# Second batch transposed in 64-column tiles without reordering copies, padding written behind the bias table, fewer 256-column units

## The chip, the cores and the metric

The kernel runs on one core of one Trainium2 chip. The metric is the device time of one execution in microseconds (us). The clock that TensorE was granted differs from one execution to the next, and this moves the time by up to about 1%. Small differences are therefore read from several rounds on one chip, never from one pair of runs. The record counts ratios within 2% as the same; smaller differences are read here from the 95% intervals.

The engines are called by their short names: PE is TensorE, PEld its weight loads, DVE is VectorE, ACT is ScalarE, POOL is GpSimd, SP is SyncE.

## The reference

Eight batches and eight heads of attention over 576 tokens, with 64 dimensions per head and a bias that depends only on the distance of query and key, are followed by a gated feed-forward layer over all 4608 tokens.

```python
scores = scale * q @ k.T                         # 8 x 8 x 576 x 576
scores = scores + bias_table[bucket(|i - j|)]    # 32 buckets, one column per head
attn   = softmax(scores)
x      = (attn @ v).transpose(...).reshape(4608, 512)
out    = ((x @ w_a) * (x @ w_b)) @ w_out         # d_ff = 1536
```

The kernel works on "pairs": pair p holds two heads of one batch, so pairs 0 to 3 are the first batch, pairs 4 to 7 the second. The 576 tokens are split in 512 and a "tail" of 64.

## The kernel before

`vt` holds the tail's values, one tile for even batches and one for odd. Head 0 of a pair lies in partitions 0 to 63, head 1 in partitions 64 to 127, each beside zeros, and each has a column of ones that gives the sum for the softmax:

```python
vt = [wpool.tile([128, H // 2, 2, Dh + 1], BF16, name=f"vt{i}") for i in range(2)]

def load_vt(b):
    for hh in range(2):
        nc.gpsimd.dma_start(
            out=vt[b % 2][64 * hh:64 * hh + 64, :, hh, 0:Dh],
            in_=v[b, hh:H:2, SM:S, :].transpose([1, 0, 2]))

def padding():
    for i in range(2):                                            # tails of q and k
        nc.vector.memset(tl[i][0:64, :, :, Dh:], 0.0)
        nc.vector.memset(tl[i][64:128, :, :, 0:Dh], 0.0)
    for i in range(2):                                            # tails of v
        nc.vector.memset(vt[i][0:64, :, 1, :], 0.0)
        nc.vector.memset(vt[i][64:128, :, 0, :], 0.0)
        nc.vector.memset(vt[i][0:64, :, 0, Dh:Dh + 1], 1.0)
        nc.vector.memset(vt[i][64:128, :, 1, Dh:Dh + 1], 1.0)
```

The order of the start, with the rest cut:

```python
nc.vector.memset(zero_sb[:, :], 0.0)
nc.vector.memset(tab_sb[0:H, :], 1.0)
nc.vector.tensor_tensor(out=bt_sb..., op=subtract)
padding()                                      # 12 memsets on DVE, ahead of all loads of q, k and v
for h in range(0, H, 2):
    load_q(0, h, h + 2)
    load_k(0, h, h + 2)
load_tails(0)
load_v(0, 0, 4)
load_vt(0)
...                                            # weights and the second batch, issued by POOL
load_vt(1)
...
warm_up(5)                                     # matmuls on zeros
nc.scalar.activation(out=eb_sb..., in_=bt_sb..., func=ACTF.Exp)
nc.tensor.matmul(out=tps..., lhsT=eb_sb..., rhs=oh_sb...)          # the bias table
warm_up(2)
nc.vector.tensor_copy(out=tab_sb[0:H, c0:c0 + NR], in_=tps[0:H, 0:NR])
nc.sync.dma_start(out=tab.ap(), in_=tab_sb[0:H, :])
for hp in range(H // 2):
    nc.sync.dma_start(out=W_sb[hp]..., in_=<a sliding view of tab>)
    if hp == 0:
        ...                                    # two loads of Wt_sb
...
t_qk(0)                                        # transposes of q and k, copies to QT and KT
t_qk(1)
scores0(0, 0)                                  # first score matmuls and exponentials
warm_up(2)
t_qk(2)
...
```

The first batch is transposed in eight 64-column matmuls per pair for each of q and k. The second batch is first brought into another order by DVE copies and is then transposed in four full ones:

```python
def transposes(ps, src, p, tag):
    b, hp = divmod(p, 4)
    for t in range(NM):
        if b == 0:
            for hh in range(2):
                o = 256 * (2 * hp + hh) + 64 * t
                nc.tensor.transpose(ps[64 * hh:64 * hh + 64, 128 * t:128 * t + 128],
                                    src[0][:, o:o + 64], ident[:, :])
        else:
            nc.tensor.transpose(ps[:, 128 * t:128 * t + 128], st[p][tag][:, t, :, :], ident[:, :])
```

The softmax here doesn't subtract the row's maximum and nothing guards it: scores larger than these inputs give would overflow.

## Time and profile before

| | before |
|---|---|
| median of 3 runs | 436.58 us (436.36 to 438.47) |
| span of the profiled run | 434.6 us, granted clock 0.998 |
| PE busy | 414.3 us, 95% |
| DVE busy, ACT busy | 242.3 us, 248.4 us |
| first score matmul | 8.87 us |

In the names of the tiles, `trq` and `trk` are transposes of q and k, `trz` those of the tails, `qkh` and `qk` scores, `av` attention times values, `pa` and `pb` feed-forward products, and `ha` the copy of `pa`.

First the page: busy time by engine, then the busy share and the granted clock of PE in 40 slices of 10.9 us, one digit each (9 is 90% or more).

```profile
PE 414.3 (95%) x3461; PEld 213.2 (49%) x3461; DVE 242.3 (56%) x596; ACT 248.4 (57%) x360; POOL 130.0 (30%) x187
...
PE   7768899999999999999999999999999999999995
...
PEclk9999999999999999999999999999999999999999
```

PE is the limit from the sixth slice on, about 55 us. Only the start has room.

Next the timeline of DVE. The columns are the start in us, the duration, the engine, the source line, the operation, output and input, and in brackets the idle time just before with what ended it.

```profile
2.75 0.27 DVE L181 MEMSET tl_99<- 64x256 uint32 x1
...
4.20 0.28 DVE L184 MEMSET vt_103<- 64x260 bf16 x1
4.57 0.28 DVE L185 MEMSET vt_103<- 64x260 bf16 x1
...
6.09 0.41 DVE L239 CAST tab_sb<-tab_ps 8x256 bf16<-8x256 f32 x1
7.66 0.42 DVE L258 COPY KT_109<-trk_232 128x512 bf16<-128x512 bf16 x1 [1.15 <-PE trk_232 L279]
...
19.80 0.69 DVE L382 TENSOR_TENSOR ath_0_0_308<-ath_0_0_308,W_89 128x1024 bf16<-128x1024 bf16 x1 [2.78 <-DMA W_89<-bias_tab]
```

The table copy (L239) runs only when the twelve memsets are done, although its matmul was over at 3.8 us. The first key copy, KT_109, waits for its transposes and for nothing else.

The waits of PE in the same kernel (engine, output, line, what it waited for; total us, times, longest us) are short:

```profile
PE trq_222 L279 <- DVE tab_sb L239: 1.8, 1, 1.8
...
PE av_0_403 L462 <- DVE vm_101 L332: 1.1, 1, 1.1
```

And four places of its PE timeline, two at the start and two in the steady part:

```profile
8.87 0.61 PE L367 MATMUL qkh_0_0_262<-QT_105,KT_109 64*128 64x256 bf16 x4
...
21.50 0.22 PE L462 MATMUL av_0_403<-vm_101,ath_0_0_272 128*128 128x65 bf16 x2 [1.15 <-DVE vm_101 L332]
...
67.46 0.38 PE L513 MATMUL pb_8_0_1253<-xn_132,wb_127 128*128 128x512 bf16 x1
67.68 0.39 PE L282 MATMUL trq_1260<-ident,qr_1198 128*128 128x128 bf16 x4
67.90 0.22 PE L458 MATMUL av_3_1268<-vt_104,att_1179 128*128 128x130 bf16 x1
```

In the steady part the start times tell more than the durations, since matmuls overlap: a 512-column matmul takes the array for 0.22 us (67.46 to 67.68), and so do four full transposes (67.68 to 67.90).

### The profile page before, as it was taken

Reading aid. Unit: us, or ns where it says so; the run is one execution under the profiler, and the core shown is the slowest. Engines: PE = TensorE matmul, PEld = TensorE weight load, DVE = VectorE, ACT = ScalarE, POOL = GpSimd, SP = SyncE. Lnnn points to the kernel's source line nnn. Section 1 sums busy time; section 2 is a strip of 40 time slices with the busy share of each in tenths; the row PEclk is TensorE's granted clock in tenths of the full one; section 3 lists DMA queues with packets and bytes.
Section 4 is the critical chain, followed back from the end, with each engine's and each line's share of the span. In section 5 each row is a group of like instructions: output and inputs, shape, how many; then the busy total and the mean of one; then the engine's idle time right before and its main releaser. Section 6 shows DMA issues by size and latency. Waiting matters only on the chain.

```text
span 434.6 us, 8819 instructions
## 1 busy us (share of the span) xinstructions
PE 414.3 (95%) x3461; PEld 213.2 (49%) x3461; DVE 242.3 (56%) x596; ACT 248.4 (57%) x360; POOL 130.0 (30%) x187
## 2 busy tenths in 40 slices
PE   7768899999999999999999999999999999999995
PEld 2456665555445544444455545454555454444442
DVE  5578688566664666467645765567546651321320
ACT  3676667666666676566656665666566632322321
POOL 9655297496009600780059003300000000000000
PEclk9999999999999999999999999999999999999999
DMA  9999999999439953997289907960420011002004
GB/s 111 213 200 184 204 118 156 147 154 173 55 63 143 164 71 63 122 156 98 51 102 163 126 15 102 150 87 14 88 81 10 15 40 72 0 3 95 1 2 97
DMA packets 138506, 42.46 MB, mean 98 GB/s; under 512 B 115896, under 2 KB 133848, under 8 KB 138464
## 3 DMA queue, kind: packets, MB, share of 16 engines
q0 software_dynamic: 81264, 18.89, 51.0%
q1 hardware_dynamic: 51760, 13.54, 20.9%
q10 hardware_dynamic: 5440, 9.47, 6.7%
q8 instruction: 27, 0.44, 0.4%
q14 instruction: 15, 0.12, 0.1%
HBM read 39.18 MB, written 9.45 MB: 112 GB/s over the span
## 4 chain that ended last, share of the span: by engine, by line
PE 85%; DVE 8%; DMA 3%; ACT 2%; issue 1%; SPq 0%; ACTq 0%; DVEq 0%
DMA W_89<-bias_tab 2%; DVE g_140 L516 1%; DMA bias_tab<-tab_sb 1%; PE po_2_1551 L523 1%; PE po_1_1477 L523 1%; PE po_1_4698 L523 1%; PE po_3_4781 L523 1%; PE po_1_4076 L523 1%; PE po_0_4013 L523 1%; PE po_1_3441 L523 1%; PE po_0_3378 L523 1%; PE po_3_2889 L523 1%; PE po_1_2806 L523 1%; PE po_1_2171 L523 1%; PE po_0_4635 L523 1%
## 5 line engine op out<-in xcount | busy, mean ns | idle before, releaser
L513 PEld LDWEIGHTS <-wb_126 128*128 128x128 bf16 x160 | 15.5, 97 | 18.2 <-issue 4.4
L503 PEld LDWEIGHTS <-wa_122 128*128 128x128 bf16 x160 | 15.1, 98 | 16.4 <-issue 1.1
L157 POOL DMA_DIRECT2D vt_104<-in_v_dram x8 | 5.0, 628 | 60.7 <-PE av_3_4083 L462 27.9
L513 PEld LDWEIGHTS <-wb_125 128*128 128x128 bf16 x160 | 13.9, 97 | 18.1 <-issue 8.0
L503 PEld LDWEIGHTS <-wa_124 128*128 128x128 bf16 x144 | 13.3, 98 | 18.3 <-issue 3.4
L503 PEld LDWEIGHTS <-wa_123 128*128 128x128 bf16 x160 | 13.9, 98 | 15.2 <-issue 3.6
L157 POOL DMA_DIRECT2D vt_103<-in_v_dram x8 | 5.0, 628 | 54.2 <-PE av_3_3448 L462 28.1
L513 PEld LDWEIGHTS <-wb_127 128*128 128x128 bf16 x144 | 12.4, 97 | 16.9 <-issue 6.7
L128 POOL DMA_DIRECT2D qn_93<-in_q_dram x24 | 18.2, 803 | 6.9 <-DMA wo<-in_moe_w_out_dram 5.7
L137 POOL DMA_DIRECT2D kn_95<-in_k_dram x24 | 18.1, 787 | 3.5 <-PE av_2_858 L458 2.3
L128 POOL DMA_DIRECT2D qn_94<-in_q_dram x24 | 18.3, 809 | 1.0 <-DMA vn_97<-in_v_dram 0.7
L137 POOL DMA_DIRECT2D kn_96<-in_k_dram x24 | 18.1, 789 | 1.4 <-DVE at_1_1220 L356 0.8
L523 PEld LDWEIGHTS <-g_137 128*128 128x128 bf16 x36 | 3.5, 97 | 9.1 <-issue 7.4
L229 PE MATMUL warm<-zero_sb 128*128 128x512 bf16 x15 | 6.3, 535 | 1.2 <-DVE zero_sb L196 1.2
L516 DVE TENSOR_TENSOR g_133<-pb_0_0_5600,ha_0_0_5598 128x512 bf16<-128x512 f32 x1 | 0.7, 692 | 11.4 <-PE pb_0_0_5600 L513 11.4
L119 POOL DMA_DIRECT2D vn_97<-in_v_dram x8 | 6.3, 783 | 0.6 <-issue 0.6
L119 POOL DMA_DIRECT2D vn_98<-in_v_dram x8 | 6.2, 780 | 0.5 <-DVE g_135 L516 0.3
L344 PEld LDWEIGHTS <-KB_116 64*128 64x128 bf16 x96 | 2.9, 94 | 7.0 <-issue 5.5
L151 POOL DMA_DIRECT2D tl_100<-in_k_dram x8 | 5.1, 659 | 3.7 <-DMA vn_97<-in_v_dram 2.2
L523 PEld LDWEIGHTS <-g_139 128*128 128x128 bf16 x36 | 3.5, 98 | 4.3
L523 PEld LDWEIGHTS <-g_135 128*128 128x128 bf16 x36 | 3.5, 98 | 4.2
L523 PEld LDWEIGHTS <-g_140 128*128 128x128 bf16 x36 | 3.5, 98 | 4.2
(3075 smaller groups left out, 1549.2 us busy)
## 6 DMA issues: line engine op xcount, KB each, us to landing
vn_97<-in_v_dram POOLq DMA_DIRECT2D x8, 256.0 KB, 6.7
vn_98<-in_v_dram POOLq DMA_DIRECT2D x8, 256.0 KB, 6.3
wo<-in_moe_w_out_dram POOLq DMA_DIRECT2D x1, 1536.0 KB, 16.6
kn_95<-in_k_dram POOLq DMA_DIRECT2D x24, 64.0 KB, 5.7
qn_93<-in_q_dram POOLq DMA_DIRECT2D x24, 64.0 KB, 5.2
kn_96<-in_k_dram POOLq DMA_DIRECT2D x24, 64.0 KB, 4.7
qn_94<-in_q_dram POOLq DMA_DIRECT2D x24, 64.0 KB, 5.0
qn_93<-in_q_dram POOLq DMA_DIRECT2D x4, 128.0 KB, 4.4
```

The costliest lines, as they stand in the source:

```text
L119: nc.gpsimd.dma_start(out=dst[:, 256 * h0:256 * h1].rearrange("p (h x) -> p h x", x=256), in_=src[b, h0:h1, 0:SM, :].rearrange("h (p t) d ...
L128: nc.gpsimd.dma_start(out=by_tile(qn[b % 2])[:, h0 // 4, t, :, :], in_=q[b, h0:h1, 128 * t:128 * t + 128, :].transpose([1, 0, 2]))
L137: nc.gpsimd.dma_start(out=by_tile(kn[b % 2])[:, h0 // 4, t, :, :], in_=k[b, h0:h1, t:SM:NM, :].transpose([1, 0, 2]))
L151: nc.gpsimd.dma_start(out=tl[b % 2][64 * hh:64 * hh + 64, :, i, Dh * hh:Dh * hh + Dh], in_=src[b, hh:H:2, SM:S, :].transpose([1, 0, 2]))
L157: nc.gpsimd.dma_start(out=vt[b % 2][64 * hh:64 * hh + 64, :, hh, 0:Dh], in_=v[b, hh:H:2, SM:S, :].transpose([1, 0, 2]))
L229: nc.tensor.matmul(out=warm[:, :], lhsT=zero_sb[:, 0:128], rhs=zero_sb[:, :], start=True, stop=True)
L344: nc.tensor.matmul(out=ps[:, hh, :], lhsT=kT[r, t, :], rhs=qT[r, :, :], start=True, stop=True)
L503: nc.tensor.matmul(out=pa[:, 0:n], lhsT=wa_sb[df // 4][:, mc, 128 * (df % 4):128 * (df % 4) + 128], rhs=xn_sb[mc][:, 512 * c + lo:512 * c ...
L513: nc.tensor.matmul(out=pb[:, 0:n], lhsT=wb_sb[df // 4][:, mc, 128 * (df % 4):128 * (df % 4) + 128], rhs=xn_sb[mc][:, 512 * c + lo:512 * c ...
L516: nc.vector.tensor_tensor(out=g_sb[df][:, lo:lo + n], in0=pb[:, 0:n], in1=ff["ha"][:, 0:n], op=MULT)
L523: nc.tensor.matmul(out=po[:, :], lhsT=g_sb[df][:, 128 * tt:128 * tt + 128], rhs=wo_sb[:, df, :], start=(df == 0), stop=(df == NDF - 1))
```

## The change

The intent has four parts. The bias table should be ready earlier, so the padding no longer stands ahead of its copy: the padding of `tl` goes to ACT, that of `vt` behind the copy on DVE. DVE loses the reordering copies of the second batch, whose transposes become eight 64-column ones like the first batch's, and the key copies of pairs 4 to 7 go to ACT. Four feed-forward groups become 512 columns wide. And there are ten exponential buffers instead of eight.

```diff
-    atp = ctx.enter_context(tc.tile_pool(name="atp", bufs=8))
+    atp = ctx.enter_context(tc.tile_pool(name="atp", bufs=10))
 ...
     def padding():
         for i in range(2):
-            nc.vector.memset(tl[i][0:64, :, :, Dh:], 0.0)
-            nc.vector.memset(tl[i][64:128, :, :, 0:Dh], 0.0)
-        for i in range(2):
             nc.vector.memset(vt[i][0:64, :, 1, :], 0.0)
             nc.vector.memset(vt[i][64:128, :, 0, :], 0.0)
             nc.vector.memset(vt[i][0:64, :, 0, Dh:Dh + 1], 1.0)
 ...
                             op=mybir.AluOpType.subtract)
-    padding()
     for h in range(0, H, 2):
         load_q(0, h, h + 2)
 ...
     nc.scalar.activation(out=eb_sb[0:NB, :], in_=bt_sb[0:NB, :], func=ACTF.Exp)
+    z = zero_sb[:, :].rearrange("p (a b c) -> p a b c", a=H // 2, b=2)
+    for i in range(2):
+        nc.scalar.activation(out=tl[i][0:64, :, :, Dh:], in_=z[0:64], func=ACTF.Copy)
+        nc.scalar.activation(out=tl[i][64:128, :, :, 0:Dh], in_=z[64:128], func=ACTF.Copy)
 ...
     nc.vector.tensor_copy(out=tab_sb[0:H, c0:c0 + NR], in_=tps[0:H, 0:NR])
+    padding()
     nc.sync.dma_start(out=tab.ap(), in_=tab_sb[0:H, :])
 ...          # the two loads of Wt now stand behind all four W loads
 ...          # reorder() and its calls removed
         for t in range(NM):
-            if b == 0:
-                for hh in range(2):
-                    ...
-            else:
-                nc.tensor.transpose(ps[:, 128 * t:128 * t + 128], st[p][tag][:, t, :, :],
-                                    ident[:, :])
+            for hh in range(2):
+                o = 256 * (2 * hp + hh) + 64 * t
+                nc.tensor.transpose(ps[64 * hh:64 * hh + 64, 128 * t:128 * t + 128],
+                                    src[b][:, o:o + 64], ident[:, :])
 ...
-            parts = [(range(0, 8), 0, 256), (range(0, 8), 256, 256), (range(8, NDF), 0, 512)]
+            parts = [(range(0, 6), 0, 256), (range(0, 6), 256, 256), (range(6, NDF), 0, 512)]
 ...
-    t_k(4)
+    t_k(4, ACT)
 ...
-    quotas = {4: 12, 5: 12, 6: 6, 7: 7, 8: 5}
+    quotas = {4: 12, 5: 8, 6: 6, 7: 6, 8: 6}
 ...          # t_k(s + 1) becomes t_k(s + 1, ACT) twice
```

More of the change, by code (lines that the diff above doesn't have):

```diff
@@ L244 @@
                                       ap=[[NM, 128], [TB, 2], [1, NY]]))
-        if hp == 0:
-            for hh in range(2):
-                nc.sync.dma_start(out=Wt_sb[64 * hh:64 * hh + 64, :, :],
-                                  in_=bass.AP(tensor=tab, offset=hh * TB + 512,
-                                              ap=[[1, 64], [2 * TB, H // 2], [1, 192]]))
+    for hh in range(2):
+        nc.sync.dma_start(out=Wt_sb[64 * hh:64 * hh + 64, :, :],
+                          in_=bass.AP(tensor=tab, offset=hh * TB + 512,
+                                      ap=[[1, 64], [2 * TB, H // 2], [1, 192]]))
     st = [dict() for _ in range(NP)]
@@ L258, in copy, with transposes @@
             nc.vector.tensor_copy(out=out, in_=in_)
-    def reorder(p):
-        b, hp = divmod(p, 4)
-        if p >= NP or b != 1:
-            return
-        for src, tag in ((qn, "qr"), (kn, "kr")):
-            r = wrk.tile([128, NM, 2, Dh], BF16, tag=tag, name=f"{tag}{p}")
-            nc.vector.tensor_copy(
-                out=r[:, :, :, :],
-                in_=src[b][:, 512 * hp:512 * hp + 512].rearrange(
-                    "p (h t d) -> p t h d", h=2, t=NM))
-            st[p][tag] = r
-    def transposes(ps, src, p, tag):
+    def transposes(ps, src, p):
         b, hp = divmod(p, 4)
         for t in range(NM):
-            if b == 0:
-                for hh in range(2):
-                    o = 256 * (2 * hp + hh) + 64 * t
-                    nc.tensor.transpose(ps[64 * hh:64 * hh + 64, 128 * t:128 * t + 128],
-                                        src[0][:, o:o + 64], ident[:, :])
-            else:
-                nc.tensor.transpose(ps[:, 128 * t:128 * t + 128], st[p][tag][:, t, :, :],
-                                    ident[:, :])
+            for hh in range(2):
+                o = 256 * (2 * hp + hh) + 64 * t
+                nc.tensor.transpose(ps[64 * hh:64 * hh + 64, 128 * t:128 * t + 128],
+                                    src[b][:, o:o + 64], ident[:, :])
     def t_q(p, eng=None):
@@ L288, in t_q @@
         ps = ps_tr.tile([128, 1024], BF16, tag="tr", name=f"trq{p}")
-        transposes(ps, qn, p, "qr")
+        transposes(ps, qn, p)
         copy(eng, QT[p % 4][:, :, :].rearrange("d a c -> d (a c)").rearrange("d (p t) -> d p t", t=NM),
@@ L296, in t_k @@
         ps = (pool or ps_tr).tile([128, 1024], BF16, tag=tag, name=f"trk{p}")
-        transposes(ps, kn, p, "kr")
+        transposes(ps, kn, p)
         copy(eng, KT[p % 4][:, :, :], ps[:, 0:SM].rearrange("d (t c) -> d t c", t=NM))
@@ L637 @@
     t_x(1, (2, 3, 4), ACT)
-    reorder(4)
     qk_half(3, 1)
@@ L666 @@
                       lambda: (qk(s, 2), ex(s, 2)), U,
-                      lambda: ex(s, 3), lambda: t_k(s + 1), U,
+                      lambda: ex(s, 3), lambda: t_k(s + 1, ACT), U,
                       lambda: mul(s, 2), U, lambda: mul(s, 3), U,
@@ L672 @@
                       lambda: mul(s, 1), A(3, 4), lambda: (qk(s, 2), ex(s, 2)), U,
-                      lambda: ex(s, 3), lambda: t_k(s + 1), U, lambda: t_x(s - 1),
+                      lambda: ex(s, 3), lambda: t_k(s + 1, ACT), U, lambda: t_x(s - 1),
                       lambda: mul(s, 2), U, lambda: mul(s, 3), U,
@@ L677 @@
             steps += [A(0, 1, 2), U, U, U, A(3, 4), U, U, U, lambda: t_x(s - 1), U, U, U]
-        reorder(s + 1)
         b = s // 4 + 1
```

## The prediction

> **What bounds the kernel now.** The page gives TensorE (PE) 95% busy. From 66 us on PE waits for almost nothing: a group of four 512-column matmuls starts every 0.86 us, and the list of waits names no later PE wait over 0.6 us. Before that PE is held up: columns streamed in the timeline, divided by 2.4 per ns (the rate of those groups), give useful work of 4.6, 7.5, 4.4, 7.3, 7.5, 8.9 and 9.1 us in the seven 10 us slices from 0 to 70, some 20 us lost. Only a shorter start or less PE work shortens the kernel.
>
> **Removed or moved earlier.**
> 1. Bias table. In the timeline the table copy on VectorE (DVE) waits behind 12 padding memsets until 6.09 us, although its matmul ends at 3.8. It should run at about 3.9. Its store starts 2.2 us earlier, and the load of W_89 also loses the two Wt issues ahead of it (1.3 us). DVE's 2.8 us wait for W_89 should vanish. PE gains less: it reaches the first attention-value group (av_0) at 20.1 us, held by a nearly continuous row of 1.02 us exponentials on ScalarE (ACT), then waits 1.15 us for vm_101. The first score chain can move only 0.2 us: the second pair's keys land at 7.96 us and their transposes already start at 8.26. Estimate: 1.4 us.
> 2. Two more exponential buffers remove ACT's 3.1 us wait at 22.2 us and PE's 0.7 us wait for xn_129, but the DVE chain behind av_0 (table products, second vm_101 copy) bounds the next step. Nothing further.
> 3. Eight reordering copies (0.27 to 0.56 us) leave DVE, and four KT copies (0.41 us) go to ACT (about 0.6). DVE is on the chain of waits at 35 to 41 and 57 to 62 us: I estimate 0.2 us at the first, limited by the av group, 0.7 at the second.
> 4. Four feed-forward groups become 512 wide: 0.86 against 2 x 0.44 us; 0.2 us in all, with fewer ACT and DVE instructions.
>
> Sum: 2.5 us.
>
> **Added.** Tail padding goes to ACT: four copies of 512 columns. The Trainium skill, "ScalarE: Activation LUTs", section "What ACT_TABLE_LOAD costs", gives 186 + 0.833 ns per element, 0.61 us; the trace's 128x512 ACT copy took 0.60. They end at about 5.2 us, before the first Q copy, and cost nothing. Transposes of pairs 4 to 7 become eight 64-column ones instead of four full ones. The first batch's run in pairs: eight take 0.25 to 0.32 us warm, four full ones 0.22. But the Trainium skill, "TensorEngine Tiling (Array Packing)", section "Key Properties", says a change of tiling mode drains the array. The trace agrees for the 64-row score matmuls: about 0.1 us is lost before and after them (at 64.2 and 64.9 us). Eight groups x 0.2 us = 1.6 us, perhaps two thirds not hidden by waits: 1.1 us. KT copies on a fuller ACT: 0.2 us.
>
> **Net**: 436.6 - 2.5 + 1.3 = 435.4; DVE's extra slack may give some more, so 434.9 us, with 433.1 to 436.4 at 8 in 10. Faster by over 2%: 0.02; within 2%: 0.96; slower by over 2%: 0.02.
>
> **What would show it.** The table copy near 4 us; no DVE wait for W_89; av_0's main matmuls near 20 us instead of 21.5; no reordering copies; a 0.1 us gap on both sides of each group of eight transposes; from 70 us the same pace, shifted by 1 to 3 us.
>
> **What would make it wrong.** Earlier table loads could delay q, k and tail loads (tails are needed at 15.2 us). The mode switch may cost nothing for column tiles, or more. The clock's warm-up at about 13 us may shift. DVE relief at 30 to 62 us may be worth 2 us more than I say.

## More of the kernel before

The padding runs without a gap, because nothing stands ahead of it.

## The result, and the profile after

| | before | after |
|---|---|---|
| median | 437.27 us, 4 runs (436.36 to 438.47) | 468.86 us, 4 runs (467.72 to 469.67) |
| ratio, 95% interval | | 1.072 (1.068 to 1.076): slower |
| span of the profiled run | 434.6 us | 467.7 us |
| granted clock of the profiled run | 0.998 | 0.996 |
| PE busy | 414.3 us | 417.8 us |
| first score matmul | 8.87 us | 39.33 us |

A ratio is the mean time of one kernel's runs over that of the other's of the same rounds, so it is not quite the ratio of the medians. The median of before has one run more here than at the time of the prediction.

PE does almost the same amount of work at the same clock, but ends 33 us later, and its first score matmul is 30.5 us late. The page shows where:

```profile
PE 417.8 (89%) x3477; PEld 212.1 (45%) x3477; DVE 237.6 (51%) x578; ACT 252.5 (54%) x366; POOL 130.1 (28%) x187
...
PE   5006688899999999999999999999999999999996
...
PEclk9999899999999999999999999999999999999999
```

The second and third slice, about 12 to 35 us, are empty. The timeline of DVE after the change shows what DVE did then:

```profile
3.85 0.41 DVE L239 CAST tab_sb<-tab_ps 8x256 bf16<-8x256 f32 x1 [0.99 <-PE tab_ps L235]
4.26 0.28 DVE L181 MEMSET vt_103<- 64x260 bf16 x1
19.46 0.28 DVE L182 MEMSET vt_103<- 64x260 bf16 x1 [14.92 <-DMA vt_103<-in_v_dram]
...
20.06 0.28 DVE L181 MEMSET vt_104<- 64x260 bf16 x1
38.31 0.28 DVE L182 MEMSET vt_104<- 64x260 bf16 x1 [17.98 <-DMA vt_104<-in_v_dram]
...
38.84 0.42 DVE L258 COPY KT_109<-trk_232 128x512 bf16<-128x512 bf16 x1
```

The table copy runs at 3.85 us, as intended. Then a memset of 0.28 us waits 14.92 us for the load into the tile that it pads, and its twin waits 17.98 us for the load into the other tile. The key copy KT_109 stands behind them in DVE's queue. It shows no wait of its own (no brackets), because its input had long been ready, as PE's timeline shows:

```profile
5.88 0.64 PE L266 MATMUL trk_232<-ident,kn_95 128*64 128x128 bf16 x8 [0.54 <-DMA kn_95<-in_k_dram]
```

The Trainium skill, "TensorE: Matmul & The Clock Gate", section "Architectural detail: the array is 16× 32×32, not 1× 128×128", says that ACT and DVE queues are strictly first in, first out; the trace agrees, since a copy that could have run at about 6.5 us ran at 38.84.

The list of waits of the changed kernel names the whole chain, in the same columns as before:

```profile
ACT ath_0_0_272 L357 <- PE qkh_0_0_262 L351: 33.7, 1, 33.7
...
PE qkh_0_0_262 L351 <- DVE KT_109 L258: 30.4, 1, 30.4
...
DVE vt_104 L182 <- DMA vt_104<-in_v_dram: 18.0, 1, 18.0
DVE vt_103 L182 <- DMA vt_103<-in_v_dram: 14.9, 1, 14.9
```

Read from the bottom, each line is the cause of one above it. DVE waits twice for a load, PE waits 30.4 us for DVE, ACT waits for PE. The chain of work that ended last (start, duration, what) crosses the same place:

```profile
28.81 0.58 POOL vt_104 L157
29.40 8.80 DMA vt_104<-in_v_dram
...
38.31 0.28 DVE vt_104 L182
...
38.84 0.44 DVE KT_109 L258
...
39.33 0.61 PE qkh_0_0_262 L351 x4
```

The load of vt_104 belongs to the second batch. POOL issues it late, behind most of the other loads, because nothing needs it early. Now the first score matmul of the first batch needs it.

Before, the padding preceded the loads in the program, so the loads kept clear of it. After, it follows them, so it must leave what they have written. Moving a memset behind a table copy has thus reversed its order against some forty loads that happen to stand between the two places, four of them into its own tiles.

The padding on ACT, in its timeline of the changed kernel, is harmless:

```profile
3.09 0.61 ACT L232 ACTIVATE tl_99<-zero_sb 64x512 bf16<-64x512 bf16 x1
...
4.99 0.63 ACT L233 ACTIVATE tl_100<-zero_sb 64x512 bf16<-64x512 bf16 x1
```

It also stands behind its loads in the program, but it waits for none of them, a difference that one experiment below explains. The Trainium skill, "ScalarE: Activation LUTs", section "What ACT_TABLE_LOAD costs", gives 186 ns and 0.833 ns per element, from which 0.61 us is estimated for 512; the trace agrees, with 0.61 to 0.63.

### The profile page after: what moved, and what is told of

Read it like the earlier page. It is cut to its first block, busy times and chain, and to the rows that moved or that the text cites. A ratio compares the mean times of both kernels' runs of the same rounds, so it can differ in the third digit from the quotient of the medians.

```text
span 467.7 us, 8822 instructions
## 1 busy us (share of the span) xinstructions
PE 417.8 (89%) x3477; PEld 212.1 (45%) x3477; DVE 237.6 (51%) x578; ACT 252.5 (54%) x366; POOL 130.1 (28%) x187
## 4 chain that ended last, share of the span: by engine, by line
PE 80%; DVE 6%; DMA 6%; ACT 3%; POOL 2%; issue 2%; ACTq 0%; DVEq 0%; POOLq 0%
DMA wb_125<-in_moe_w_b_dram 2%; DMA vt_104<-in_v_dram 2%; DMA tl_99<-in_q_dram 1%; DVE g_140 L500 1%; POOL qn_93 L119 1%; POOL kn_95 L119 1%; PE po_2_1575 L507 1%; PE po_0_1445 L507 1%; PE po_0_2098 L507 1%; PE po_3_4771 L507 1%; PE po_1_4688 L507 1%; PE po_3_4149 L507 1%; PE po_1_4066 L507 1%; PE po_0_4003 L507 1%; PE po_1_3431 L507 1%
## 5 line engine op out<-in xcount | busy, mean ns | idle before, releaser
L351 PE MATMUL qkh_0_0_262<-QT_105,KT_109 64*128 64x256 bf16 x4 | 0.6, 404 | 30.4 <-DVE KT_109 L258 30.4
L497 PEld LDWEIGHTS <-wb_126 128*128 128x128 bf16 x152 | 14.5, 97 | 19.0 <-issue 4.6
L487 PEld LDWEIGHTS <-wa_122 128*128 128x128 bf16 x160 | 15.1, 98 | 17.2 <-issue 2.0
L497 PEld LDWEIGHTS <-wb_125 128*128 128x128 bf16 x160 | 14.0, 97 | 18.1 <-issue 8.0
L487 PEld LDWEIGHTS <-wa_124 128*128 128x128 bf16 x144 | 13.3, 98 | 18.3 <-issue 3.4
L487 PEld LDWEIGHTS <-wa_123 128*128 128x128 bf16 x152 | 13.2, 98 | 15.3 <-issue 3.6
L497 PEld LDWEIGHTS <-wb_127 128*128 128x128 bf16 x144 | 12.4, 97 | 16.6 <-issue 6.3
L357 ACT ACTIVATE ath_0_0_272<-qkh_0_0_262 128x1024 bf16<-128x1024 f32 x1 | 1.0, 1024 | 33.7 <-PE qkh_0_0_262 L351 33.7
L137 POOL DMA_DIRECT2D kn_95<-in_k_dram x24 | 18.1, 795 | 3.5 <-PE qkh_0_0_298 L351 1.8
L137 POOL DMA_DIRECT2D kn_96<-in_k_dram x24 | 18.1, 785 | 2.0 <-PE trk_946 L266 2.0
L351 PEld LDWEIGHTS <-KT_109 64*128 64x128 bf16 x16 | 0.8, 111 | 32.0 <-DVE KT_109 L258 30.7
L182 DVE MEMSET vt_103<- 64x260 bf16 x1 | 0.3, 275 | 14.9 <-DMA vt_103<-in_v_dram 14.9
L507 PEld LDWEIGHTS <-g_137 128*128 128x128 bf16 x36 | 3.5, 97 | 8.7 <-issue 6.8
```

Of the source, the lines that this page charges most:

```text
L137: nc.gpsimd.dma_start(out=by_tile(kn[b % 2])[:, h0 // 4, t, :, :], in_=k[b, h0:h1, t:SM:NM, :].transpose([1, 0, 2]))
L351: nc.tensor.matmul(out=ps[:, hh, 256 * e:256 * e + 256], lhsT=kT[r, 2 * u + e, :], rhs=qT[r, 2 * h:2 * h + 2, :], start=True, stop=True)
L357: nc.scalar.activation(out=at[:, :, :], in_=st[p]["ps", h, u][:, :, :], func=ACTF.Exp, scale=scale)
L487: nc.tensor.matmul(out=pa[:, 0:n], lhsT=wa_sb[df // 4][:, mc, 128 * (df % 4):128 * (df % 4) + 128], rhs=xn_sb[mc][:, 512 * c + lo:512 * c ...
L497: nc.tensor.matmul(out=pb[:, 0:n], lhsT=wb_sb[df // 4][:, mc, 128 * (df % 4):128 * (df % 4) + 128], rhs=xn_sb[mc][:, 512 * c + lo:512 * c ...
L507: nc.tensor.matmul(out=po[:, :], lhsT=g_sb[df][:, 128 * tt:128 * tt + 128], rhs=wo_sb[:, df, :], start=(df == 0), stop=(df == NDF - 1))
```

## The experiments

**Theory A**: the moved padding of `vt` waits for the loads into its own tiles, and DVE's queue holds the key copies behind it. **Rivals**: the loss comes from the earlier table loads, which crowd out the inputs (B), from the other parts of the change (C), or from the granted clock (D). D is weak from the start: the clocks of the two profiled runs were 0.998 and 0.996.

Every run is compared with runs of the kernel before on its own chip. The first four, e1, e2, e3 and e5, shared one, e8, e10, e11 and e12 another, e4, e14 and the repeat of e12 a third; e15 had a fourth. Versions on different chips (e2 with e8 and e11, e14 with e15) are set side by side by their ratios only.

### e1: the moved padding alone

```diff
 # against the kernel before
     def padding():
         ...                       # the four memsets of tl, at their old place
+    def padding_vt():
         ...                       # the eight memsets of vt
 ...
     nc.vector.tensor_copy(out=tab_sb[0:H, c0:c0 + NR], in_=tps[0:H, 0:NR])
+    padding_vt()
```

> The kernel before with one edit: the eight memsets that pad the two value-tail tiles run behind the copy of the bias table, and so stand in program order behind the loads that fill those tiles. Theory A (the loss is a wait of VectorE, in its queue's order, for those two loads, and everything behind it is late): the profile has two waits on VectorE of about 15 and 18 us before the padding of the two tiles, the first score matmul starts near 39 us, and the time is 465 to 470 us. Theory B (the loss comes from the other parts: 64-column transposes, copies on ScalarE, earlier table loads competing with the input loads): 435 to 438 us, like the kernel before.

Measured: 465.91 us against 437.67, ratio 1.065 (1.063 to 1.067). This one move makes 28.2 us of the loss. Its list of waits has both DVE waits in one line (32.7 us in two waits):

```profile
DVE vt L187 <- DMA vt<-in_v_dram: 32.7, 2, 17.7
```

Two of its runs had a mean clock of 1.000 and still took 465.8 and 466.0 us, and one with a mean of 0.958 took 465.8 too. So D falls. C falls too as the main cause, since none of the other parts is in this kernel, and so does B for the bulk of it, unless the table loads starve the inputs by themselves; e2 looks at that. The rest of the difference to the changed kernel, some 3 us, was measured in different rounds. The traces show that it does not arise at the start: the first score matmuls of pair 4 stand at 74.35 us here and at 74.38 in the changed kernel, those of pair 6 at 95.36 and 96.10, and the spans end at 465.7 and 467.7. A part of it turns up again under e15.

### e2: the changed kernel, with the loads written behind the padding

```diff
 # against the kernel after
-    for h in range(0, H, 2):          # the whole block of input loads
-        load_q(0, h, h + 2)
-        ...
 ...
     padding()
+    for h in range(0, H, 2):          # the same block, here
+        load_q(0, h, h + 2)
+        ...
     nc.sync.dma_start(out=tab.ap(), in_=tab_sb[0:H, :])
```

> The changed kernel, whole, but the block of input loads is written behind the padding, so that the loads wait for the padding and not the padding for the loads. The order on each engine's queue is the same. Theory A: no DMA wait before the padding, first score matmul near 8.7 us, 433 to 436.5 us, as I had predicted for the change itself. Theory B: still 465 us or more.

Measured: 440.29 us against 437.67, ratio 1.006 (1.003 to 1.010). The stall is gone, which A requires: nothing but the order of the program changed. The expected gain is missing, however: the time lies outside both expected ranges, and the kernel is slightly slower than before. So a second, smaller loss was hidden under the first. The PE timeline of this run shows it:

```profile
15.75 0.22 PE L287 MATMUL trz<-ident,tl 128*128 128x128 bf16 x1 [1.14 <-DMA tl<-in_q_dram]
17.64 0.70 PE L287 MATMUL trz<-ident,tl 128*128 128x128 bf16 x7 [1.68 <-DMA tl<-in_k_dram]
```

PE waits for the tails of q and k, the last of which landed at 17.6 us instead of 12.2. In exchange the table loads start at 6.75 us instead of 10.47. This is the first risk that the prediction named, and B in small. The Trainium skill, "Trainium Kernel Development and Optimization", section "Key Constraints", says that DMAs from all queues run on the same 16 engines and interleave; the trace agrees, in that the last of the four loads of the tails took 8.8 us from issue to landing instead of 3.3 while four table loads of 290 KB were under way.

Then something is added. (The record of the clock is not whole at the start: in the kernel before it reads 1.00 from 10 to 12 us, while eight transposes took 0.43 us there and 0.25 after 13 us. So the clock is read here only from 13 us on.) These are two stretches of 10 us on PE in e2: stretch, length, PE busy (instructions), granted clock, and two columns on the DMA that are not used here.

```profile
10.00:20.00 10.00, 5.85 (x68) 0.84 1.34 222
20.00:30.00 10.00, 8.16 (x83) 0.50 1.36 195
```

The second of the two stretches, in the kernel before:

```profile
20.00:30.00 10.00, 5.83 (x110) 1.00 1.34 208
```

From about 18 us, in the thin stretch, the clock fell to half, and it stayed there for the whole of the next. PE was busy for more of it and did fewer instructions, 83 instead of 110: a busy PE is not always a fast one. The Trainium skill, "TensorE: Matmul & The Clock Gate", Part 1, says that the clock falls to half after an idle window of about 3.4 us, and that this window runs freely, so that the moment varies from run to run. The trace agrees with the half (0.50). It shows no single gap of that length, however: the longest waits of PE before the fall are the 1.14 and 1.68 us above, with one matmul between them. What set off the fall is therefore not shown. That it varies fits the six executions of e2, which took 437.9 us (clock 0.999) to 442.65 us (0.988).

### e3: one of the two tiles padded ahead of the loads

```diff
 # against the kernel after
+    padding((1,))                     # vt[1], ahead of the loads
     for h in range(0, H, 2):
         load_q(0, h, h + 2)
 ...
-    padding()
+    padding((0,))                     # vt[0], behind the table copy
```

> The changed kernel, but only the first value-tail tile is padded behind the bias table and the loads; the second is padded ahead of them. Theory A: VectorE waits only for the first tile's load (it landed at 19.5 us in the changed kernel), the first score matmul starts near 20.5 us instead of 39.3, some 11.5 us later than in the kernel before, of which a little may be won back because the tables are there by then: 444 to 449 us. Theory B: 465 us or more.

Measured: 450.48 us against 437.67, ratio 1.029 (1.026 to 1.031), slightly above the expected range. DVE's timeline shows one wait in place of two:

```profile
19.74 0.28 DVE L182 MEMSET vt<- 64x260 bf16 x1 [15.21 <-DMA vt<-in_v_dram]
...
20.28 0.42 DVE L259 COPY KT<-trk 128x512 bf16<-128x512 bf16 x1
```

The key copy runs at 20.28 us instead of 38.84, and the time falls with it: the stall is as long as the later of the loads that the padding waits for. The rest of the kernel, the earlier table loads included, is as in the changed one.

### e5: the changed kernel, with the padding of vt at its old place

```diff
 # against the kernel after
+    padding()
     for h in range(0, H, 2):
         load_q(0, h, h + 2)
 ...
     nc.vector.tensor_copy(out=tab_sb[0:H, c0:c0 + NR], in_=tps[0:H, 0:NR])
-    padding()
```

> The changed kernel with the eight value-tail memsets at their old place, ahead of the loads and of the table copy. Theory A: no such wait, the table copy at about 4.8 us (between 3.9 and 6.1), 433.5 to 437 us, at most 1 us slower than with the loads written behind the padding. Theory B: 465 us or more.

Measured: 437.55 us against 437.67, ratio 1.000 (0.998 to 1.002), 0.6 us above the expected range. All the rest of the change together neither costs nor gains. Together with e1 this settles where the 31.6 us are: in the place of eight memsets. It also puts the rest of the prediction below what was hoped, since part of the earlier table is in this version (the copy runs at 4.63 us, W loads at 8.97). The score matmuls of pair 4 started 1.07 us earlier than before, and this was lost again by the end.

### e8: e2 with more warm-up matmuls

```diff
 # against e2
     scores0(2, 0)
-    warm_up(2)
+    warm_up(10)
     t_tails0()
```

> e2_loads_behind with eight more warm-up matmuls (1.7 us at full rate) in front of the tail transposes, which wait for the tails anyway. If the half clock is most of the loss of that kernel, its matmuls from 17.6 to 31 us now run at full rate and it takes 436 to 438.5 us; if the wait for the tails alone is, it stays at 440 us.

Measured: 439.26 us against 438.5, ratio 1.002 (0.998 to 1.006). In the profiled run the clock was below full only from 20.6 to 24 us, but the tails also came earlier than in e2, so two things differ. This run is inconclusive. It didn't show that filling the wait with warm-up buys anything.

### e10: the transposes of the second batch alone

```diff
 # against the kernel before
-    def reorder(p): ...
     def transposes(ps, src, p, tag):  # eight 64-column transposes for both batches
 ...
-    reorder(4)
-        reorder(s + 1)
```

> The kernel before with one part of the change: no reordering copies, 64-column transposes for the second batch. Theory E: 0.3 to 1.2 us slower than the kernel before (1.6 us of mode switches, less up to 0.9 us of VectorE time). The intent of the change: 0.5 to 1 us faster.

Measured: 438.21 us against 438.5, ratio 0.999 (0.996 to 1.002). The time decides between neither of the expectations. The PE timeline does show the cost of the switch:

```profile
68.70 1.02 PE L497 MATMUL pb<-xn,wb 128*128 128x512 bf16 x4
69.66 0.41 PE L266 MATMUL trq<-ident,qn 128*64 128x128 bf16 x8
70.00 0.23 PE L442 MATMUL av<-vt,att 128*128 128x130 bf16 x1
```

Four 512-column matmuls keep the array for 0.86 us, here until 69.56. The transposes start at 69.66, 0.10 later, and the next matmul 0.34 after them: 0.44 us for the group. In the kernel before it was 0.22. The Trainium skill, "TensorEngine Tiling (Array Packing)", section "Key Properties", says that a change of tiling mode drains the array; the trace agrees, and gives the figure that the page doesn't have. What the eight groups lose, DVE's relief seems to give back.

### e11: e2, with the last table loads held back

A memset of one element of the third table tile is put behind the copies of the third pair. Two tables and the two loads of Wt are written behind it, so that the two tables are issued from 12.2 us and Wt from 13.1, and not right behind the first two tables (7.9 us).

```diff
 # against e2
-    ...                               # W_sb[2], W_sb[3] and Wt loaded with the first two
     t_qk(2)
+    nc.vector.memset(W_sb[2][0:1, 0, 0:1], 0.0)
+    load_W(nc.sync, 2)
+    load_W(nc.sync, 3)
+    load_Wt(nc.sync)
     scores0(1, 0)
```

> The changed kernel with the loads behind the padding (as in e2_loads_behind), and besides the loads of the third and fourth bias table and of the tail table are held back to about 11.3 us, behind the third pair's query copy. Theory C (what kept e2_loads_behind from the predicted gain is that its table loads, begun at 6.75 us, delayed the q, k and tail loads: the tails landed at 17.6 us instead of 12.2, PE stood still for 2.8 us and its clock then fell to half until about 31 us): the tails land by 15.5 us, no PE wait for them, no half-rate matmuls after 15 us, and 434.5 to 436.5 us. Theory D (it is the added PE work of the narrower transposes and the fuller ScalarE): no better than e2_loads_behind, 438 us or more.

Measured: 436.86 us against 438.5, ratio 0.997 (0.995 to 1.000), 0.4 us above the expected range. The tail transposes ran at 14.83 us without a wait, so the loss of e2 did come from the early table loads. The expectation of a full clock after 15 us failed: in the profiled run it was below full for parts of 19 to 33 us. In the profiled run of the kernel before it did not fall anywhere from 13 to 46 us. So the wait for the tails is not needed for such a fall, and what is stays open.

### e12 and its repeat: e11 with the full transposes kept

```diff
 # against e11
+    def reorder(p): ...               # as in the kernel before
     ...                               # full transposes of the second batch, as before
```

> e11_tables_staged with the reordering copies and the full 128-column transposes of the kernel before put back. Theory E (the narrower transposes cost about 0.2 us of mode switch per group of eight, 1.6 us in all, more than the copies that they save on VectorE are worth): 0.5 to 1.5 us faster than e11_tables_staged. The intent of the change (VectorE bounds this stage and the copies are worth more): 0.5 to 1 us slower.

Measured: 436.06 us against 438.5, ratio 0.995 (0.992 to 0.997). This is 0.8 us less than e11 on the same chip, in the direction and of the size expected, but the two intervals overlap, so this cost of the 64-column transposes is likely and not shown.

> The kernel of e12_staged_full_transposes once more, on the same chip as e14_order_only: 0.3 to 0.8 per cent faster than the kernel before, if its gain of 0.54 per cent was no accident of the chip and of the clock's falls.

Measured on the third chip: 436.47 us against 437.76, ratio 0.997 (0.994 to 1.001). The gain of 0.3% is at the lower edge of what was expected, and the interval includes no gain at all.

### e4: two columns decide

Why did only some memsets wait? The padding and the loads never touch the same element. A half of `vt` is 65 columns of two bytes, 130 bytes, which is not a multiple of four. In the upper partitions the zeros end with column 64, bytes 128 and 129 of the row, and the first loaded value sits in bytes 130 and 131: the same four-byte word. The column of ones of the upper half (bytes 258 and 259) shares a word with the last loaded value. The other two memsets share no word with any load, and nor do those of `tl`, whose halves are 64 columns wide. They had no wait. (The single-column memsets stand behind the one that waited, so for them the trace decides nothing.) In e4 only those two columns are padded ahead of the loads, and everything else stays behind them:

```diff
 # against the kernel after
     def padding():
         for i in range(2):
             nc.vector.memset(vt[i][0:64, :, 1, :], 0.0)
-            nc.vector.memset(vt[i][64:128, :, 0, :], 0.0)
+            nc.vector.memset(vt[i][64:128, :, 0, 0:Dh], 0.0)
             nc.vector.memset(vt[i][0:64, :, 0, Dh:Dh + 1], 1.0)
+
+    def padding_edge():
+        for i in range(2):
+            nc.vector.memset(vt[i][64:128, :, 0, Dh:Dh + 1], 0.0)
             nc.vector.memset(vt[i][64:128, :, 1, Dh:Dh + 1], 1.0)
 ...
+    padding_edge()
     for h in range(0, H, 2):
         load_q(0, h, h + 2)
```

> The changed kernel; of the value-tail padding only the four tiny memsets of single columns in the upper half of the partitions (column 64 of the first head, column 129) go ahead of the loads; the large memsets stay behind the table copy and behind the loads in program order, with column 64 cut off the one that waited. If the wait hung on that one column alone, which ends two bytes before the loaded region begins and shares a four-byte word with its first element, the large memsets no longer wait for any load: no DMA wait on VectorE before the first key copy, and 437 to 441 us, like e2_loads_behind and e5_pad_old_place. If any memset of these tiles behind the loads waits for them, 465 us or more.

Measured: 439.58 us against 437.76, ratio 1.003 (0.998 to 1.008). DVE has no wait for a load any more, although the large memsets stand behind the loads just as in the changed kernel. From its DVE timeline:

```profile
4.62 0.27 DVE L182 MEMSET vt<- 64x256 bf16 x1
...
5.67 0.42 DVE L263 COPY KT<-trk 128x512 bf16<-128x512 bf16 x1
```

The memset that waited until 19.46 us runs at 4.62 once its last column is cut off (64x256 elements instead of 64x260). So the 32.9 us of DVE's waits were put in for these two columns, or for one of them; they were moved together. That the rule goes by words of four bytes fits all eight memsets of `vt` and the padding of `tl`, but other tile widths were not tried. Whether the chip itself would need the wait is not shown either; no version that drops the wait alone was run.

### e14: the order alone, done right

The last question was whether the intent of the change can be had. e14 is the kernel before with its transposes, its copies, its buffers and its units, and only the order is new: the table chain first, then the padding, then the loads, with the last tables held back as in e11.

```diff
 # against the kernel before
-    padding()
-    ...                               # all input loads
     warm_up(5)
     ...                               # exponential and matmul of the table
     nc.vector.tensor_copy(out=tab_sb[0:H, c0:c0 + NR], in_=tps[0:H, 0:NR])
+    padding()
     nc.sync.dma_start(out=tab.ap(), in_=tab_sb[0:H, :])
+    load_W(nc.sync, 0)
+    load_W(nc.sync, 1)
+    ...                               # all input loads
 ...
     t_qk(2)
+    nc.vector.memset(W_sb[2][0:1, 0, 0:1], 0.0)
+    load_W(nc.sync, 2)
+    load_W(nc.sync, 3)
+    load_Wt(nc.sync)
```

> The kernel before with the order alone changed, nothing of the transposes, ScalarE copies, buffers or units: all padding behind the table copy, the loads written behind the padding, the tables staged as in e11_tables_staged. If the useful part of the change is the earlier table (1.4 us in my prediction), 0.5 to 1.8 us faster than the kernel before and within 1 us of e12; if it is the rest, no faster than the kernel before.

Measured: 434.65 us (434.33 to 436.04) against 437.76, ratio 0.993 (0.990 to 0.997). The gain is larger than the 0.5 to 1.8 us expected, and e12 is more than 1 us away. With e15 this is the fastest version, and it beats both given kernels. The lines that answer to those of before, one of DVE and one of PE, are:

```profile
3.84 0.41 DVE L214 CAST tab_sb<-tab_ps 8x256 bf16<-8x256 f32 x1 [1.10 <-PE tab_ps L210]
...
7.60 0.42 DVE L263 COPY KT<-trk 128x512 bf16<-128x512 bf16 x1
...
20.18 0.42 PE L467 MATMUL av<-vm,ath 128*128 128x65 bf16 x8
```

The first attention-value group starts at 20.18 us instead of 21.50, as the prediction had it (20.1), and the score matmuls of pair 4 at 41.66 instead of 43.15. DVE's product with the second table, which had waited 2.78 us for W_89 and run at 19.80, runs at 16.59 without a wait, also as predicted. The gain of 1.3 us at the first place and 1.5 at the second is kept: the span is 1.9 us shorter. Part of the 3.1 us between the medians goes with the clock. On that chip the kernel before took 435.43 and 435.93 us in its two executions at clock 1.000, and up to 440.14 at 0.980; e14 was at 0.992 or above in all six. At clock 1.000 alone the difference of the means is about 1.1 us (435.7 against 434.5). Whether e14 falls to half clock less often because of its order is not shown by six executions.

### e15: e14 with the units of the change

```diff
 # against e14
-            parts = [(range(0, 8), 0, 256), (range(0, 8), 256, 256), (range(8, NDF), 0, 512)]
+            parts = [(range(0, 6), 0, 256), (range(0, 6), 256, 256), (range(6, NDF), 0, 512)]
 ...
-    quotas = {4: 12, 5: 12, 6: 6, 7: 7, 8: 5}
+    quotas = {4: 12, 5: 8, 6: 6, 7: 6, 8: 6}
```

> The kernel of e14_order_only with one more part of the change: fewer 256-column feed-forward units and the quotas that go with them. My prediction gave this part 0.2 us of gain: 434 to 434.6 us, if the order's gain is as in e14_order_only. The traces of e12 against e14 suggest the opposite: e12 is 0.5 us ahead when the second batch begins and 0.3 us behind ten microseconds later, so if the units are the reason this run is 0.5 to 1 us slower than e14_order_only was against the kernel before, a ratio of 0.995 to 0.997 instead of 0.993.

Measured: 434.82 us against 437.96, ratio 0.994 (0.991 to 0.996), which can't be told from e14; the predicted 0.2 us is too small for these intervals. e12, which has the same order of tables and loads and the same transposes as e14, is 1.8 us slower on the same chip (436.47 against 434.65). The units alone did not show such a loss, so what is left is the padding on ACT, the key copies on ACT, the ten buffers, or the units together with one of these.

The traces narrow this down. From the first score matmuls of pair 4 to those of pair 6, 20.99 us pass in e14, 21.03 in e15, 21.10 in the kernel before, but 21.50 in the repeat of e12, 21.72 in e11 and in the changed kernel, and 21.73 in e5. ACT's timeline in the repeat of e12 shows the key copy of pair 5 right ahead of a feed-forward copy, and the list of PE's waits shows PE waiting for that copy:

```profile
50.72 0.65 ACT L262 ACTIVATE KT<-trk 128x512 bf16<-128x512 bf16 x1
51.20 0.45 ACT L513 ACTIVATE ha<-pa 128x256 f32<-128x256 f32 x1
...
PE pa L509 <- ACT ha L513: 0.6, 1, 0.6
```

The changed kernel, e5 and e11 have the same wait of 0.6 us; the kernel before, e1, e10, e14 and e15, whose key copies are on DVE, have none in this stretch. So the key copies on ACT explain about 0.6 of the 1.8 us, as far as traces can show it; no run with them alone was made. The rest stays open.

## Why the prediction was wrong

**The step that failed is the first one, "Bias table".** It said that the table copy waits behind the padding and, with the padding moved, "should run at about 3.9". That was right (3.85). What it left out is the other end of the move: where the memsets land, what they then stand behind, and what stands behind them. In the sum, the moved memsets count as nothing. The runs put a term of +30.4 us there, PE's wait for KT_109. With it, the predicted -1.7 us becomes about +29 of the measured +31.6, and e1, with nothing else changed, measured +28.2 by itself. The list "What would make it wrong" has no entry for it either. It could have been had without a run: the compiled program lists the waits of each instruction, and there the memset of `vt` in the changed kernel has a wait for a DMA that it didn't have before. (In the changed kernel the second memset of each tile waits for a DMA semaphore, in the kernel before and in e4 none of them does.)

**The size of the table's gain** (1.4 us) was right where it was predicted: e14, with the order repaired, has 1.3 us at the first attention-value group and 1.5 us at pair 4. At the end it is about 1.1 us between the few executions at clock 1.000.

**"Earlier table loads could delay q, k and tail loads"** was named as a risk and came true. In e2 the tails landed 5.4 us late and the kernel lost its gain; e11 took the cause away and part of it came back. In the changed kernel the tails' loads of k are late too (a median of 7.7 us from issue to landing, 3.5 before), but it costs nothing there, since everything waits for DVE anyway.

**The mode switch** of the 64-column transposes was estimated at 0.2 us per group and measured 0.22. That about 1.1 us of it reach the end is not shown: the 0.8 us between e11 and e12 are what is left after DVE's relief, and the two intervals overlap.

**The padding on ACT** cost PE nothing at the start, as predicted: it ended at 5.62 us and QT_105 ran at 5.64.

**The key copies on ACT** were put at 0.2 us in all; one of them alone makes PE wait 0.6 us. What else makes up the 1.8 us between e12 and e14 is open.

**The 0.2 us from the wider units and the 0.9 us from DVE's relief** did not show. e15 can't be told from e14, and e5, with all of the rest in it, is at 1.000.

**PE's steady pace** from 70 us on was predicted to stay and did; the timeline is shifted there by +32 us instead of -1 to -3.

## What to carry to other kernels

When an instruction is moved, look at both ends: what it no longer blocks at the old place, and at the new place everything between the two that touches the same tile, since the order against each of those is reversed. A cheap instruction in a queue that runs in order is as expensive as the longest wait it can catch, so list the waits of the moved instructions in the compiled program before any time is predicted. And when a start-up chain is made faster, hold back the transfers that nobody needs yet, or they take the earlier start away from those that somebody does.

## What the Trainium skill lacked or had wrong

- No page was found that says that a wait can be put in between a memset and a load that touch no common element, where they share a four-byte word. Here it cost 14.9 and 18.0 us on DVE, and cutting off one column of 65 and moving another took it away (e4). "SBUF — State Buffer" would be the place.
- "TensorEngine Tiling (Array Packing)", "Key Properties", says that a change of mode drains the array and gives no figure. Here a group of eight 64-column transposes between full-size matmuls takes 0.44 us against 0.22 for four full ones: 0.10 us lost ahead of it, 0.12 in it or behind it (e10, and the same in the changed kernel at 99.64 us).
- "TensorE: Matmul & The Clock Gate", Part 1, ties the fall of the clock to an idle window of about 3.4 us. Here it fell with no PE wait of that length: in e2 the longest wait before the fall was 1.68 us, and in the profiled run of e11 it fell at about 19 us, where PE had waited 0.6 us at most since 13 us.
- "Trainium Kernel Development and Optimization", "Key Constraints", says that all queues share the DMA engines, which agrees, but not how much a small load suffers: with four table loads of 290 KB beside it the last 32 KB load of the tails took 8.8 us instead of 3.3 (e2).
